# Two first blocks of a short convolution on TensorE, W_in swapped across partitions by TensorE, dummy products during the loads, and two more short blocks

## Chip, cores and metric

The kernel runs on one core of a Trainium2 chip. The metric is the device time of one execution in microseconds (us); "span" is the length of the one profiled execution and is 1.7 to 2.4 us shorter than the time of the same execution. All runs here are of state fast. Engines: TensorE (PE, with PEld for its weight loads), VectorE (DVE), ScalarE (ACT), GpSimd (POOL), and SyncE (SP), whose queue issues most DMAs.

## The reference

A causal convolution over time with 7 taps, whose weights are a softmax per head (8 heads of 24 channels), and after it a two-layer network with exact gelu:

```python
w = exp(weight - max); w = w / (sum(w) + 1e-9)          # weight: [8, 7]
y[b, s, ch] = sum_k w[head(ch), k] * x_pad[b, s + k, ch] # x: [8, 4096, 192], f32
out = gelu(y.reshape(32768, 192) @ w_in) @ w_out         # w_in: [192, 2048], w_out: [2048, 192]
```

## The kernel before

The tokens are cut into two halves of 16384, one half on partitions 0 to 63 and the other on 64 to 127, and each half into blocks. For each block n, VectorE transposes the input and does the convolution (21 instructions over three channel groups p), TensorE multiplies by W_in (`mm1`), ScalarE applies gelu, TensorE multiplies by W_out (`mm2`, of the block before, interleaved with `mm1`), VectorE copies the result out of PSUM (`evac`), and SyncE's queue stores it.

```python
WS = [256, 256] + [512] * ((HALF - 512) // 512)     # tokens per block
...
def conv(n, k, p):                                  # VectorE, k = 0..6, p = 0..2
    src = ap(xT[n % 2], p * XW + 32 * kt, [[NP * XW, 128], [1, w]])
    if k == 0:
        ins = v.tensor_scalar(a, src, wk, None, ALU.mult)
    else:
        ins = v.scalar_tensor_tensor(dst, src, wk, a, op0=ALU.mult, op1=ALU.add)
...
for n in range(NB):                                 # TensorE
    todo = units(n - 1) if n >= 1 else []           # mm2 of the block before
    for i in range(NSL[n]):
        mm1(n, i)                                   # waits for all of conv(n) at i == 0
        for un in todo[a0:a1]:
            mm2(n - 1, *un)
...
sp.dma_start(wsb[:, :], ap(wt, 0, [[KS, H], [1, KS]])).then_inc(S_WSB, 16)   # SyncE's queue
load(sp, 0, (0, 1)); load(sp, 1, (0, 1))
sp.wait_ge(S_WIN[1], 32)
for hf, c0, c1 in ((1, FC, FM), (0, FM, F)):        # the other half of W_in, SBUF to SBUF
    sp.dma_start(win[other half] <- win[this half]).then_inc(S_WIN[2], 16)   # (abridged)
load(sp, 2)
for n in range(1, NB):
    if n + 2 < NB:
        load(sp, n + 2)
    store(sp, n - 1)                                # waits for evac of block n-1
```

## Time and profile before

| | before |
|---|---|
| time, median of 4 | 703.43 us |
| span of the profiled execution | 702.0 us |
| first `mm1` | 15.8 us |
| VectorE starts block 2, has it ready | 28.08 us, 43.7 us |
| TensorE then works until | 698.6 us |

First, lines of the profile page: busy time per engine, and from its part 4 the chain that ended last as shares of the span.

```profile
span 702.0 us, 24852 instructions
...
PE 675.1 (96%) x11366; PEld 517.8 (74%) x11366; DVE 563.0 (80%) x925; ACT 526.3 (75%) x516; POOL 37.2 (5%) x78
...
PE 91%; DVE 4%; DMA 3%; SPq 1%; issue 1%; POOL 0%; POOLq 0%
```

The windows view gives the busy time of each engine in a stretch, then granted TensorE clock, DMA share and GB/s.

```profile
core 0: us, PE busy (x) PEld busy (x) DVE busy (x) ACT busy (x) POOL busy (x), PEclk, DMA share, GB/s
0.00:16.00 16.00, 1.61 (x10) 1.54 (x12) 10.71 (x31) 2.96 (x4) 6.44 (x15) 1.00 1.08 197
16.00:24.00 8.00, 4.32 (x42) 2.90 (x40) 7.96 (x22) 2.32 (x3) 0.87 (x2) 1.00 1.13 239
24.00:32.00 8.00, 7.14 (x122) 5.45 (x120) 5.10 (x11) 7.45 (x8) 1.01 (x2) 1.00 1.01 212
32.00:45.00 13.00, 9.08 (x180) 8.23 (x178) 13.00 (x21) 6.63 (x8) 0.00 (x0) 1.00 0.11 23
...
100.00:200.00 100.00, 100.00 (x1688) 76.49 (x1686) 83.75 (x135) 78.18 (x78) 4.73 (x10) 1.00 0.53 120
```

From 100 us on TensorE is busy all the time; before 45 us it is not, and up to 32 us the DMA engines are full. The timeline (start, length, instruction, and in brackets the idle time before it and what ended it) shows who sets the start. VectorE:

```profile
23.95 1.26 DVE L303 SCALAR_TENSOR_TENSOR xc<-xT,wcol,acc 128x256 bf16<-128x256 f32 x3
28.08 1.90 DVE L273 STREAM_TRANSPOSE xT<-xin 128x512 f32<-128x512 f32 x3 [2.87 <-DMA xin<-in_x_dram]
30.01 1.75 DVE L296 TENSOR_SCALAR acc<-xT,wcol 128x512 f32<-128x512 f32 x3
31.68 10.02 DVE L303 SCALAR_TENSOR_TENSOR acc<-xT,wcol,acc 128x512 f32<-128x512 f32 x15
41.62 2.07 DVE L303 SCALAR_TENSOR_TENSOR xc<-xT,wcol,acc 128x512 bf16<-128x512 f32 x3
```

And TensorE, same view:

```profile
43.83 0.82 PE L423 MATMUL hp<-xc,win 64*128 64x512 bf16 x6 [2.05 <-DVE xc L303]
```

TensorE waits until VectorE has block 2 ready at 43.7 us and is the limit from there to the end. An earlier first matmul is worth something only if it moves such a ready time.

### The profile page before, as it was taken

The numbers are of one execution on the slowest core, as the hardware profiler recorded it, in microseconds if no ns is written. First come the engines' busy times: TensorE is split into PE (matmuls) and PEld (weight loads), VectorE is DVE, ScalarE is ACT, GpSimd is POOL, SyncE is SP. The second block draws the span as 40 slices with busy tenths as digits, with TensorE's granted clock in tenths as the row PEclk, the third lists the DMA queues.
The fourth block names the chain that finished last, engine by engine and source line by source line (L and its number), as shares of the span: only waits on it lengthen the run. The fifth ranks groups of instructions, "written<-read, shape, count | busy, mean of one in ns | idle before, by whom it ended". The sixth has DMA issues, their size and how long they took to land.

```text
span 702.0 us, 24852 instructions
## 1 busy us (share of the span) xinstructions
PE 675.1 (96%) x11366; PEld 517.8 (74%) x11366; DVE 563.0 (80%) x925; ACT 526.3 (75%) x516; POOL 37.2 (5%) x78
## 2 busy tenths in 40 slices
PE   1779999999999999999999999999999999999998
PEld 1566777777777777777777777777777777777777
DVE  6899888988888988888988888898888898888811
ACT  1668777777777777777777777777777777777771
POOL 4000000000000000000000000000000000000000
PEclk9999999999999999999999999999999999999999
DMA  9925545565434665334555444556443566543113
GB/s 203 198 64 116 118 85 117 136 135 122 97 84 107 137 136 132 93 88 97 136 136 134 91 101 89 131 135 135 107 96 84 123 135 137 115 97 77 31 47 93
DMA packets 21929, 78.92 MB, mean 112 GB/s; under 512 B 6720, under 2 KB 9920, under 8 KB 17856
## 3 DMA queue, kind: packets, MB, share of 16 engines
q1 hardware_dynamic: 18096, 74.50, 47.2%
q0 software_dynamic: 2896, 1.67, 1.7%
q8 instruction: 89, 1.46, 0.9%
q10 hardware_dynamic: 832, 1.16, 0.6%
q14 instruction: 16, 0.13, 0.1%
HBM read 53.13 MB, written 25.17 MB: 112 GB/s over the span
## 4 chain that ended last, share of the span: by engine, by line
PE 91%; DVE 4%; DMA 3%; SPq 1%; issue 1%; POOL 0%; POOLq 0%
PE ob L455 47%; PE hp L423 44%; DVE acc L303 3%; DMA xin<-in_x_dram 1%; DMA win<-in_moe_w_in_dram 1%; DVE xT L273 0%; DVE xc L303 0%; DVE acc L296 0%; SPq L130 0%; DVE osb L312 0%; POOL win L229 0%; SPq L495 0%; POOL win L236 0%; POOL sel L185 0%; POOL sel L195 0%
## 5 line engine op out<-in xcount | busy, mean ns | idle before, releaser
L380 ACT ACTIVATE gT<-hp 128x1024 bf16<-128x1024 f32 x512 | 523.4, 1024 | 160.4 <-PE hp L423 160.3
L423 PE MATMUL hp<-xc,win 64*128 64x512 bf16 (+1 forms) x3168 | 425.9, 372 | 19.3 <-DVE xc L303 12.9
L455 PEld LDWEIGHTS ob<-wout,gT 64*128 64x128 bf16 x8192 | 369.1, 94 | 101.9
L455 PE MATMUL ob<-wout,gT 64*128 64x192 bf16 x8192 | 428.6, 243 | 0.0
L303 DVE SCALAR_TENSOR_TENSOR acc<-xT,wcol,acc 128x512 f32<-128x512 f32 (+1 forms) x495 | 326.9, 725 | 0.0
L423 PEld LDWEIGHTS hp<-xc,win 64*128 64x128 bf16 x3168 | 162.9, 95 | 74.6 <-issue 19.2
L312 DVE COPY osb<-ob 128x384 f32<-128x384 f32 x128 | 70.2, 550 | 126.9 <-PE ob L455 126.9
L303 DVE SCALAR_TENSOR_TENSOR xc<-xT,wcol,acc 128x512 bf16<-128x512 f32 (+1 forms) x99 | 66.6, 726 | 0.0
L273 DVE STREAM_TRANSPOSE xT<-xin 128x512 f32<-128x512 f32 (+1 forms) x99 | 60.7, 664 | 3.1 <-DMA xin<-in_x_dram 3.1
L296 DVE TENSOR_SCALAR acc<-xT,wcol 128x512 f32<-128x512 f32 (+1 forms) x99 | 57.1, 629 | 1.2
L223 POOL COPY xT<-xT 128x558 f32<-128x558 f32 x33 | 21.5, 652 | 611.4 <-DVE xT L273 611.4
L214 POOL COPY xT<-xT 128x18 f32<-128x18 f32 x29 | 11.6, 400 | 0.0
L394 PE MATMUL ob<-wnm,sel 8*128 8x7 f32 x6 | 1.4, 354 | 4.2 <-DVE wnm L258 4.2
L394 PEld LDWEIGHTS ob<-wnm,sel 8*128 8x128 f32 x6 | 1.4, 321 | 4.2 <-issue 4.2
L356 ACT ACT_TABLE_LOAD x1 | 1.3, 1283 | 1.7 <-PEq L521 1.7
L250 DVE TENSOR_REDUCE wmx<-wsb 8x1 f32<-8x7 f32 x1 | 0.1, 148 | 2.2 <-DMA wsb<-in_weight_dram 2.2
L262 DVE COPY wcol<-ob 128x21 f32<-128x21 f32 x1 | 0.2, 181 | 1.6 <-PE ob L394 1.6
L229 POOL DMA_DIRECT2D win<-in_moe_w_in_dram x2 | 1.4, 688 | 0.0
L380 ACT ACT_TABLE_LOAD x1 | 1.3, 1283 | 0.0
L236 POOL DMA_DIRECT2D win<-in_moe_w_in_dram x2 | 1.2, 627 | 0.0
L240 POOL DMA_DIRECT2D wout<-in_moe_w_out_dram x1 | 1.2, 1192 | 0.0
L254 DVE TENSOR_SCALAR wsm<-wsm 8x1 f32<-8x1 f32 x1 | 0.1, 142 | 1.1 <-ACT wex L356 1.1
(12 smaller groups left out, 3.3 us busy)
## 6 DMA issues: line engine op xcount, KB each, us to landing
xin<-in_x_dram SPq DMA_DIRECT2D x124, 380.0 KB, 7.1
out_dram<-osb SPq DMA_DIRECT2D x120, 192.0 KB, 3.1
out_dram<-osb SPq DMA_DIRECT2D x24, 48.0 KB, 1.7
wout<-in_moe_w_out_dram POOLq DMA_DIRECT2D x1, 768.0 KB, 13.0
xin<-in_x_dram ACTq DMA_DIRECT2D x4, 188.0 KB, 4.5
xin<-in_x_dram SPq DMA_DIRECT2D x4, 188.0 KB, 4.8
win<-in_moe_w_in_dram POOLq DMA_DIRECT2D x2, 336.0 KB, 8.4
win<-win SPq DMA_DIRECT2D x2, 336.0 KB, 6.3
```

The source lines that it names most:

```text
L214: g.tensor_copy(dst, ap(xT[(n - 1) % 2], WS[n - 1] + 31, [[NP * XW, 128], [XW, NP], [32, HB]],),).then_inc(S_HALO)
L223: g.tensor_copy(ap(xT[n % 2], 1, [[NP * XW, 128], [XW, NP], [32, HB], [1, 31]]), ap(xT[n % 2], WS[n], [[NP * XW, 128], [XW, NP], [32, HB], ...
L229: g.dma_start(ap(win, 64 * hf * NP * F, [[NP * F, 64], [F, NP], [1, FC]]), ap(wint, 0, [[F, 64], [64 * F, NP], [1, FC]]),).then_inc(S_WIN[ ...
L273: v.transpose(ap(xT[n % 2], p * XW + HL, [[NP * XW, 128], [1, w]]), ap(xin[n % NX], 64 * p, [[TB // 32 * D, 128], [D, w // 32], [1, 32]],) ...
L296: ins = v.tensor_scalar(a, src, wk, None, ALU.mult)
L303: ins = v.scalar_tensor_tensor(dst, src, wk, a, op0=ALU.mult, op1=ALU.add)
L312: v.tensor_copy(ap(osb[m % 2], g * C, [[8 * C, 128], [4 * C, 2], [1, C]]), ap(ob[(G0[m] + g) % 2], 0, [[1024, 128], [512, 2], [1, C]]),).t ...
L356: a.activation(out=wex[:, :], in_=wsb[:, :], func=AF.Exp, bias=wmx[:, 0:1], accum_out=wsm[:, 0:1],).then_inc(S_ACTP)
L380: a.activation(out=ap(gT[n % 2], i * c * 2 * w, dst), in_=ap(hp[u % 2], 0, src), func=AF.Gelu,).then_inc(S_GELU)
L394: ins = t.matmul(ob[0][:, p * KS : (p + 1) * KS], sel[:, p * 128 : (p + 1) * 128], wnm[:, :],)
L423: ins = t.matmul(hp[u % 2][:, hf * TB + cc * w : hf * TB + cc * w + w], win[r, p * F + f0 : p * F + f0 + 128], xc[n % 2][r, p * TB : p * T ...
L455: ins = t.matmul(ob[gg % 2][:, 512 * sub : 512 * sub + C], gT[m % 2][r, c0 : c0 + 128], wout[r, i * C : (i + 1) * C], start=(ph == 0 and i ...
```

## The change

Its intent is to use the idle first 45 us better. The convolution of blocks 0 and 1 becomes TensorE products with diagonal matrices (7 per channel group and half); the half of W_in that each partition half lacks is fetched by TensorE products with an identity and copied out of PSUM by VectorE, in place of DMAs; 22 dummy products run while the first loads are under way. Blocks 2 and 3 also shrink from 512 to 256 tokens, and the softmax is computed on all 128 partitions. Core of the diff, with cuts marked by `...`:

```diff
-    WS = [256, 256] + [512] * ((HALF - 512) // 512)
+    WS = [256] * 4 + [512] * ((HALF - 1024) // 512)
+    ND = 2
...
+            def diag(p):                                     # VectorE
+                v.tensor_tensor(dg, idn, wcol, ALU.mult)     # abridged
+            def dup_out(s):                                  # VectorE, 4 x
+                v.tensor_copy(win[.., FH + s * FQ ..], DUPB[s])   # abridged
...
+            late = {(0, 0): (2, 18), (0, 1): (3, 8), (1, 0): (3, 20), (1, 1): (4, 6)}
+            late.update({(2, 0): (4, 13), (2, 1): (4, 21)})   # (block, group): evac before (block, op)
...
+            t.wait_ge(S_WARM, 1)                             # TensorE
+            for i in range(22):
+                t.matmul(hp[1][:, 0:512], warm[:, 0:128], warm[:, :])
+            def dup(s): ...      # win halves times identity, into PSUM
+            def pconv(n, p): ... # 7 taps x 2 halves: dg[..] times xTb[..], into PSUM
+            pconv(0, 0)
+            pconv(0, 1)
+            dup(0)
+            pconv(0, 2)
+            behind = {1: [(dup, 1)], 2: [(dup, 2)], 3: [(dup, 3)]}  # after mm1(0, i)
+            for p in range(NP):
+                behind[4 + p] = [(pconv, 1, p)]
...
-            sp.dma_start(wsb[:, :], ap(wt, 0, [[KS, H], [1, KS]])).then_inc(S_WSB, 16)
+            sp.dma_start(wsb[:, :], ap(wt, 0, [[0, 128], [1, H * KS]])).then_inc(S_WSB, 16)
             load(sp, 0, (0, 1))
-            load(sp, 1, (0, 1))
-            sp.wait_ge(S_WIN[1], 32)
-            for hf, c0, c1 in ((1, FC, FM), (0, FM, F)):
-                sp.dma_start( ... win <- win ... ).then_inc(S_WIN[2], 16)
+            sp.wait_ge(S_WIN[0], 32)
+            load(sp, 1)
             load(sp, 2)
+            sp.wait_ge(S_WOUT, 16)
             for n in range(1, NB):
                 if n + 2 < NB:
                     load(sp, n + 2)
                 store(sp, n - 1)
```

The loop on SyncE's queue is unchanged: block 4's load stands behind the stores of block 0. The table `late` fixes where in VectorE's program each evacuation stands.

## The prediction

> **What bounds the kernel now.** From about 44 us on, TensorE: the windows view gives PE 100% busy in every 100 us stretch from 100 to 600 us, at 20.95 us per 512-token block. Before that VectorE sets the start: the chain of waits runs through input DMA, then VectorE's third convolution (28.08 to 43.7 us), and from 43.83 us through TensorE alone until 698.6 us; evacuation and store add 3.4 us. The first gelu matmul starts at 15.8 us, but only blocks 0 and 1 profit. So the end is "VectorE finishes block k's convolution" plus TensorE's remaining work: 43.8 + 31 x 20.95 + 5.2 = 698.5. The change is worth only what it moves these ready times.
>
> **What changes.** Removed from VectorE: 42 convolution steps on 256 columns (9.5 us per block with transposes). Added: three diagonal builds (est. 0.6 us each, from 0.40 us at 256 columns and 0.68 at 512), four weight copies out of PSUM (est. 0.9 us each, from 0.47 at 384), casts and copies. The W_in swap by DMA (336 KB x 2, 6.3 us) goes; the same DMA engines carry all early loads (the Trainium skill, "DMA: Bandwidth & Descriptors", Issuing engines are not separate DMA queues; the trace agrees: 190 to 277 GB/s shared until 32 us), so inputs land sooner. But blocks 2 and 3 shrink to 256: together 19 us on VectorE where one 512 block costs 15.5.
>
> **Estimated timeline.** First gelu matmul at 11.2 us. Block 0 then waits for weight copies; block 1's last convolution copy ends about 21.5 us, by which time block 2's input should have landed (before: 28.06). Call VectorE's start of block 2 s = 21.5. With evacuations, block 2 is ready at s+10, block 3 at s+20.5. Block 4's load stands behind the stores of block 0, which wait for an evacuation placed inside block 3: it issues about s+16 and needs 8.1 us (measured: first issue 48.9, last landing 57.0). VectorE waits 3 to 4 us; block 4 is ready at s+41 = 62.7. TensorE's work left is then 30 x 20.95 + 5.2 = 633.7, ending at 696.4.
>
> TensorE runs dry near 53 us and idles 9 us. The Trainium skill, "TensorE: Matmul & The Clock Gate", Part 1, says that an idle window of about 3.4 us halves the clock until about as long a busy time; the trace has the first 12 matmuls after idling take 1.46 us where 0.83 is usual. Estimated cost 1 to 2 us. The dummy products let the first matmuls run warm, under 1 us and off the later chain.
>
> Net: -6.6 (earlier s), +0.5 (short blocks), +3.5 (late load), +1.5 (cold clock): -1, or better where these overlap. From block 6 on nothing changes.
>
> **Prediction: 701.5 us**, 8 in 10 between 697.0 and 705.0. Faster by over 2%: 0.01; within 2%: 0.97; slower by over 2%: 0.02.
>
> **Right if:** first gelu matmul at 10 to 13 us; VectorE's first transpose of block 2 at 20 to 24; a VectorE wait for input of 2 to 6 us before block 4's transposes; a TensorE gap of 6 to 12 us ending at 60 to 65, released by VectorE's convolution; then 20.95 us per block, unchanged.
>
> **Wrong if:** weight halves land after 13 us (s goes to 25, the end past 704); block 4's load lands in time (3 to 4 us better); PSUM copies or diagonal builds cost twice my estimate; W_out lands after 23 us and stalls block 1.

## The result, and the profile after

The changed kernel takes 709.16 us (median of 4, 707.68 to 709.73); before it is 703.43. The ratio is 1.0079, with a 95% interval from 1.0061 to 1.0096. (Ratios here are the mean time of one kernel's fast runs over the mean of the other's in the same rounds, so not quite the ratio of the medians quoted.) It is slower by under 1%, and outside the range of 697 to 705.

The page of the kernel after:

```profile
span 706.7 us, 25342 instructions
...
PE 687.9 (97%) x11586; PEld 521.2 (74%) x11586; DVE 558.5 (79%) x924; ACT 528.4 (75%) x523; POOL 39.0 (6%) x90
...
PE 92%; DVE 5%; DMA 2%; issue 1%; SPq 0%; ACT 0%; ACTq 0%
```

Its windows view (columns as above):

```profile
0.00:16.00 16.00, 11.72 (x96) 6.68 (x98) 5.99 (x16) 6.04 (x12) 7.15 (x23) 0.89 0.95 180
16.00:24.00 8.00, 6.55 (x102) 4.48 (x102) 5.10 (x11) 5.42 (x6) 1.22 (x4) 1.00 0.98 175
...
32.00:45.00 13.00, 12.93 (x276) 12.02 (x274) 12.96 (x33) 9.42 (x10) 0.87 (x2) 1.00 0.36 91
45.00:60.00 15.00, 13.61 (x294) 13.17 (x289) 10.44 (x19) 10.45 (x11) 1.01 (x2) 1.00 0.52 120
60.00:100.00 40.00, 32.36 (x473) 22.00 (x470) 37.83 (x61) 27.06 (x28) 2.01 (x4) 0.91 0.57 124
100.00:200.00 100.00, 100.00 (x1686) 75.24 (x1684) 82.64 (x134) 78.39 (x77) 4.74 (x10) 1.00 0.50 116
```

TensorE is far busier before 45 us (6.3 of the 11.7 us in the first row are dummies), nothing of note differs from 100 us on, and there is a new loss between 45 and 100 us: VectorE works only 10.44 of 15 us, TensorE 32.36 of the next 40, at a mean clock of 0.91. The timeline of VectorE shows the first part of it:

```profile
25.78 1.09 DVE L396 STREAM_TRANSPOSE xT<-xin 128x256 f32<-128x256 f32 x3
...
45.10 1.27 DVE L426 SCALAR_TENSOR_TENSOR xc<-xT,wcol,acc 128x256 bf16<-128x256 f32 x3
50.90 1.90 DVE L396 STREAM_TRANSPOSE xT<-xin 128x512 f32<-128x512 f32 x3 [4.53 <-DMA xin<-in_x_dram]
```

VectorE starts block 2 at 25.78 us (before: 28.08), is done with block 3 at 46.37 us, and then waits 4.53 us for block 4's input. SyncE's queue, same view, shows why that was late; L185 is the stores, L171 the load:

```profile
33.58 7.75 SPq L185 DMA_DIRECT2D out_dram<-osb  x8
41.38 1.81 SPq L171 DMA_DIRECT2D xin<-in_x_dram  x4
```

The load is issued right after the stores of block 0, whose second group waits for an evacuation at 39.03 us. TensorE in the same view runs dry in the meantime:

```profile
68.05 1.46 PE L611 MATMUL hp<-xc,win 64*128 64x512 bf16 x6 [7.64 <-DVE xc L426]
```

These six matmuls take 1.46 us, where the same six took 0.82 us in the kernel before at 43.83 us. The windows view with finer stretches shows the clock there, and around the first convolutions:

```profile
10.00:11.00 1.00, 0.91 (x16) 0.91 (x18) 0.23 (x1) 0.68 (x3) 0.84 (x3) 0.94 1.10 145
11.00:14.00 3.00, 3.00 (x36) 2.21 (x32) 0.96 (x1) 0.77 (x2) 0.00 (x0) 0.50 1.39 246
...
66.00:72.00 6.00, 3.95 (x30) 2.48 (x32) 5.96 (x10) 1.55 (x2) 1.00 (x2) 0.50 0.73 168
72.00:73.00 1.00, 1.00 (x16) 0.53 (x12) 1.00 (x3) 0.55 (x2) 0.00 (x0) 0.83 1.07 243
```

The granted clock is 0.50 between 11 and 14 us and from 66 to 72 us. The first of these stretches meets the opening convolutions, which come 2.54 us after the last dummy:

```profile
1.26 6.29 PE L535 MATMUL hp<-warm 128*128 128x512 bf16 x22 [1.26 <-DVE warm L316]
10.09 1.82 PE L575 MATMUL ob<-xTb,dg 64*64 64x256 bf16 x22 [2.54 <-ACT xTb L493]
```

The theory from this: the end is a chain of (1) VectorE's start of block 2, (2) its work up to block 4, (3) the late load, (4) TensorE's remaining work from block 4 on, (5) with a stretch at half clock. Rivals were that the wait is slack and something steady got slower; that the short blocks or the W_in swap are the cost; and that the slow matmuls are no matter of clock.

### The profile page after: what moved, and what is told of

The parts are those of the page before. It is cut to its first block, busy times and chain, and to the rows that moved or that the text cites. A ratio compares the mean times of both kernels' runs of the same rounds, so it can differ in the third digit from the quotient of the medians.

```text
span 706.7 us, 25342 instructions
## 1 busy us (share of the span) xinstructions
PE 687.9 (97%) x11586; PEld 521.2 (74%) x11586; DVE 558.5 (79%) x924; ACT 528.4 (75%) x523; POOL 39.0 (6%) x90
## 4 chain that ended last, share of the span: by engine, by line
PE 92%; DVE 5%; DMA 2%; issue 1%; SPq 0%; ACT 0%; ACTq 0%
PE ob L643 46%; PE hp L611 45%; DVE acc L426 2%; DMA xin<-in_x_dram 1%; PE ob L575 1%; DVE xT L396 1%; DMA wsb<-in_weight_dram 1%; DVE acc L419 1%; DVE xc L426 0%; DVE osb L435 0%; DVE dg L357 0%; SPq L185 0%; SPq L171 0%; DVE win L367 0%; PE ob L551 0%
## 5 line engine op out<-in xcount | busy, mean ns | idle before, releaser
L643 PEld LDWEIGHTS ob<-wout,gT 64*128 64x128 bf16 x8192 | 363.9, 94 | 106.5 <-issue 2.5
L426 DVE SCALAR_TENSOR_TENSOR acc<-xT,wcol,acc 128x512 f32<-128x512 f32 (+1 forms) x480 | 316.9, 722 | 0.0
L426 DVE SCALAR_TENSOR_TENSOR xc<-xT,wcol,acc 128x512 bf16<-128x512 f32 (+1 forms) x96 | 64.5, 723 | 0.0
L289 POOL COPY xT<-xT 128x18 f32<-128x18 f32 x29 | 11.5, 396 | 0.0
L575 PE MATMUL ob<-xTb,dg 64*64 64x256 bf16 x84 | 6.8, 321 | 2.8 <-ACT xTb L493 2.5
L575 PEld LDWEIGHTS ob<-xTb,dg 64*64 64x64 bf16 x84 | 5.2, 126 | 4.4 <-ACT xTb L493 3.0
L535 PE MATMUL hp<-warm 128*128 128x512 bf16 x22 | 6.3, 454 | 1.3 <-DVE warm L316 1.3
L367 DVE CAST win<-ob 128x768 bf16<-128x768 f32 x3 | 2.9, 952 | 4.3 <-PE ob L551 4.3
L535 PEld LDWEIGHTS hp<-warm 128*128 128x128 bf16 x22 | 2.4, 114 | 4.6 <-issue 1.9
(35 smaller groups left out, 20.4 us busy)
## 6 DMA issues: line engine op xcount, KB each, us to landing
wout<-in_moe_w_out_dram POOLq DMA_DIRECT2D x1, 768.0 KB, 15.6
```

The lines of the kernel that those rows point to most:

```text
L289: g.tensor_copy(dst, ap(xT[(n - 1) % 2], WS[n - 1] + 31, [[NP * XW, 128], [XW, NP], [32, HB]],),).then_inc(S_HALO)
L367: v.tensor_copy(ap(win, FH + s * FQ, [[NP * F, 128], [F, NP], [1, FQ]]), ap(DUPB[s], 0, [[1024, 128], [FQ, NP], [1, FQ]]),).then_inc(S_DUPE)
L535: t.matmul(hp[1][:, 0:512], warm[:, 0:128], warm[:, :])
L575: ins = t.matmul(b[r, o : o + w], dg[r, d0 : d0 + 64], xTb[n][r, x0 : x0 + w], start=(k == KS - 1), stop=(k == 0), tile_position=(64 * hf, ...
L643: ins = t.matmul(ob[gg % 2][:, 512 * sub : 512 * sub + C], gT[m % 2][r, c0 : c0 + 128], wout[r, CH[i] * C : (CH[i] + 1) * C], start=(ph == ...
```

## The experiments

Eleven kernels ran, all correct. "Start of block 2", "wait" (VectorE, for block 4's input) and "block 4" (TensorE's first matmul of it) are from each profile's timeline, "end" is the start of the last evacuation, all in us. The column "rest" is end minus block 4, that is, TensorE's work from there on.

The experiments ran in three sessions on three chips: a, b, d, e; then c, f, g, j; then m, k, l. The kernel before ran in each of them, with medians of 704.15, 704.00 and 703.36 us. So a difference between medians of two sessions can be off by 0.8 us; the ratios don't have this fault, and where they say something else it is noted. Where a difference is read from profiles, it is one execution against one.

| run | median (runs) | ratio to before | start of block 2 | wait | block 4 | end | rest |
|---|---|---|---|---|---|---|---|
| before | 703.43 (4) | 1 | 28.08 | | | 698.65 | |
| after | 709.16 (4) | 1.0079 | 25.78 | 4.53 | 68.05 | 703.23 | 635.2 |
| m_again | 709.05 (5) | 1.0083 | 24.30 | 4.80 | 66.83 | 702.38 | 635.6 |
| a_ahead | 702.87 (5) | 0.9993 | 24.39 | none | 62.04 | 697.71 | 635.7 |
| e_keepwarm | 705.94 (5) | 1.0027 | 24.30 | 4.5 | 66.44 | 699.53 | 633.1 |
| j_ahead_keep | 701.70 (5) | 0.9969 | 24.31 | none | 62.83 | 695.93 | 633.1 |
| f_blocks | 703.08 (5) | 0.9993 | 25.07 | none | | 697.39 | |
| b_warm33 | 708.52 (5) | 1.0062 | 24.31 | 4.9 | 66.93 | 703.15 | 636.2 |
| c_warm0 | 711.11 (4) | 1.0102 | 26.09 | 5.81 | 69.64 | 705.38 | 635.7 |
| d_wsbfirst | 709.30 (5) | 1.0076 | 25.21 | 5.5 | 68.44 | 703.33 | 634.9 |
| g_swapdma | 716.71 (4) | 1.0179 | 32.21 | 5.50 | 75.46 | 711.06 | 635.6 |
| k_wsbrow | 707.73 (5) | 1.0056 | 23.52 | 4.96 | 66.20 | 702.06 | 635.9 |
| l_best | 700.16 (5) | 0.9953 | 22.79 | none | 60.79 | 693.88 | 633.1 |

### m_again: the changed kernel once more

No edit. Expected:

> The changed kernel itself once more, on the same chip as the two runs beside it. Its first profile had the opening convolutions at half clock (VectorE's block 2 at 25.8 us); three variants with the same opening did not (24.3 us). If that is chance from execution to execution, its times scatter over some 2 us between 707.5 and 710, and this profile has block 2 at 24.3 or 25.8 us, with the same 4.5 to 5.5 us wait for block 4's input and half clock after it.

Measured: 708.18 to 709.86, and block 2 at 24.30 us. TensorE's and VectorE's timelines:

```profile
1.26 7.76 PE L535 MATMUL hp<-warm 128*128 128x512 bf16 x22 [1.26 <-DVE warm L316]
10.08 1.39 PE L575 MATMUL ob<-xTb,dg 64*64 64x256 bf16 x22 [1.07 <-ACT xTb L493]
```

```profile
24.30 1.09 DVE L396 STREAM_TRANSPOSE xT<-xin 128x256 f32<-128x256 f32 x3
```

So of two profiles of one program, one has the opening convolutions at half clock and one has not, and that is worth 1.5 us of block 2's start. The timelines show where they part: the 22 dummies took 7.76 us here and 6.29 us in the first profile (633 against 379 ns each in the median), so the gap between them and the convolutions was 1.07 us here and 2.54 us there. The wait (4.80 us) and the half clock before block 4 are in both. The times spread over 1.7 us here and from 707.68 to 709.73 us in the first result; how many of these executions opened at half clock is not known, for only one of each set was profiled.

### a_ahead: the input loads one block earlier

```diff
+            load(sp, 3)
             for n in range(1, NB):
-                if n + 2 < NB:
-                    load(sp, n + 2)
+                if n + 3 < NB:
+                    load(sp, n + 3)
                 store(sp, n - 1)
```

> The changed kernel, with every input load from block 4 on issued one block earlier, ahead of the stores that it stood behind. Theory (a chain: VectorE start of block 2, late load of block 4, cold TensorE clock): VectorE's 4.5 us wait for block 4's input goes, block 4 is ready at about 63.4 us instead of 67.9, TensorE's gap shrinks from 7.6 to about 3 us and the half-clock stretch after it mostly goes; time falls by 4.5 to 6 us, to about 703 to 704.5. Rival 1 (the steady state or TensorE's own start is the limit, and the wait is slack): within 1 us of 709. Rival 2 (the earlier load collides with other transfers and another wait takes its place): the wait goes, but less than 3 us is gained.

Measured: 702.87, 6.2 us less than m_again, at the upper edge of what was expected and a little beyond; the spans of the two profiles differ by 4.3 us. The wait is gone (VectorE's line has no idle time before it), and TensorE's gap is 4.59 us in place of 7.6 to 8.2. VectorE first, then TensorE:

```profile
44.90 1.89 DVE L396 STREAM_TRANSPOSE xT<-xin 128x512 f32<-128x512 f32 x3
```

```profile
62.04 1.47 PE L611 MATMUL hp<-xc,win 64*128 64x512 bf16 x6 [4.59 <-DVE xc L426]
```

The wait was on the chain; that is shown, and the rest from block 4 on is as before (635.7 against 635.6 us in m_again), so the gain lies ahead of block 4. One part of the expectation failed: the half clock did not go with the shorter gap. The windows view of this run has it still:

```profile
60.00:62.00 2.00, 0.00 (x0) 0.00 (x0) 2.00 (x4) 0.00 (x0) 0.00 (x0) 0.62 0.42 114
62.00:66.00 4.00, 3.96 (x30) 2.49 (x32) 3.96 (x7) 1.56 (x2) 1.01 (x2) 0.50 0.83 183
66.00:68.00 2.00, 2.00 (x22) 1.03 (x18) 2.00 (x4) 1.10 (x2) 0.00 (x0) 0.67 1.02 219
```

### e_keepwarm: dummy products in the gap before block 4

```diff
+                if i == 0 and n == 4:
+                    for _ in range(30):
+                        t.matmul(hp[u % 2][:, 0:512], warm[:, 0:128], warm[:, :])
                 if i == 0:
```

> The changed kernel with 30 dummy products on TensorE put into its gap before block 4 (about 6.5 us of the 7.6 us gap). Theory: the half clock from 65.5 to 72.3 us in the records costs about 1.6 us of TensorE work on the chain; with the gap filled the clock stays full and the time falls by 1.2 to 1.8 us to about 707.5. Rival: the slow matmuls after the gap are a start-up effect of the block or wait on other engines; no change (709), or worse by the overlap if the dummy products outlast the gap.

Measured: 705.94, 3.1 us less than m_again (3.9 us by the ratios), about twice what was expected or more. TensorE's timeline and then the windows view of this run:

```profile
58.99 6.65 PE L601 MATMUL hp<-warm 128*128 128x512 bf16 x30
66.44 0.82 PE L614 MATMUL hp<-xc,win 64*128 64x512 bf16 x6 [0.81 <-DVE xc L426]
```

```profile
62.00:66.00 4.00, 3.63 (x17) 1.47 (x15) 4.00 (x7) 0.00 (x0) 0.00 (x0) 1.00 0.59 136
66.00:72.00 6.00, 5.56 (x78) 3.28 (x80) 5.96 (x11) 4.70 (x5) 1.00 (x2) 1.00 0.90 209
```

The six matmuls take 0.82 us again, the clock stays at 1.00, and the rest from block 4 on is 633.1 us in place of 634.9 to 636.2 us in the eight profiles without filled gaps (after, m_again, a, b, c, d, g, k). So the half clock costs 1.8 to 3.1 us here, 2.1 in the first profile after. The clock record gives the same size by another way. Take TensorE's busy time from block 4 on in windows of 0.5 us, times the share of the clock that was not granted: the sum is 2.1 us in the first profile after, 1.9 to 2.8 us in all eight, and zero in e_keepwarm. The last evacuation starts at these times in the view of the chain (start, length, what), m_again first and then e_keepwarm:

```profile
702.38 0.56 DVE osb L435
```

```profile
699.53 0.56 DVE osb L435
```

The Trainium skill, "TensorE: Matmul & The Clock Gate", Part 1 (What's actually happening), names the mechanism, a clock halved after idling; pace, record and remedy agree with it.

### j_ahead_keep: both repairs

The edits of a_ahead and e_keepwarm, with 18 dummies.

> Both repairs together: input loads one block earlier, and 18 dummy products (3.9 us) in the 4.6 us gap that TensorE still has before block 4. The first run with earlier loads still showed half clock from 60.8 to 67.4 us. Theory: the two costs add up, so the time falls by a further 3 us from 702.9, to 699.5 to 700.5, below the kernel before. Rival: they overlap or the steady state takes it back; 702 or more.

Measured: 701.70, ratio 0.9969 (0.9957 to 0.9982): below the kernel before, but 1.2 us above the expected band. The dummies outlast the gap by 0.8 us (block 4 ready at 62.0, first matmul at 62.83). The two gains add up in large part: 7.4 us together against 9.3 for the sum of the two alone (8.0 and 10.2 by the ratios), and 6.5 against 7.5 us in the ends of the profiles. The surplus dummies are 0.8 us of what is missing; the other 0.2 to 1.4 us can be overlap or scatter.

### f_blocks: the block sizes of before

```diff
-    WS = [256] * 4 + [512] * ((HALF - 1024) // 512)
+    WS = [256] * 2 + [512] * ((HALF - 512) // 512)
...
-            late = {(0, 0): (2, 18), (0, 1): (3, 8), (1, 0): (3, 20), (1, 1): (4, 6)}
-            late.update({(2, 0): (4, 13), (2, 1): (4, 21)})
-            for n in range(3, NB):
+            late = {(0, 0): (2, 12), (0, 1): (2, 20), (1, 0): (3, 16), (1, 1): (4, 0)}
+            for n in range(2, NB):
```

> The changed kernel with two 256-token blocks and then 512 (as before), instead of four, evacuations placed to suit; load order as in the changed kernel. Theory: block 4's late load disappears (the load after block 0's stores is then wanted only some 16 us later); VectorE starts block 2 at 24.3 to 25.8 us and has it ready 16.5 us later, at 41 to 42.5; 654.9 us of TensorE work follow. TensorE runs dry for 3 to 5 us before it, with up to 3 us of half clock. Time 700.5 to 705, that is 4 to 8 us below the changed kernel. Rival (the short blocks 2 and 3 themselves help by feeding TensorE in smaller pieces): 708 or more.

Measured: 703.08, as expected. VectorE starts block 2 at 25.07 us, TensorE's block 2 starts at 42.11 us:

```profile
42.11 1.46 PE L610 MATMUL hp<-xc,win 64*128 64x512 bf16 x6 [4.31 <-DVE xc L426]
```

With two long blocks in place of four short ones the same load order costs nothing, since the load behind the stores is wanted some 15 us later (VectorE takes block 4 at 59.70 us, and would have taken it at 44.9 us in m_again). The half clock is here too, but shorter: after the gap of 4.31 us it costs 1.3 us by the clock record. So the late load and the short blocks are one cause: the shorter blocks brought the need forward, and the load order did not follow. This is also the change without its block sizes: level with the kernel before (0.9979 to 1.0006).

### b_warm33 and c_warm0: more dummies, no dummies

`range(22)` becomes `range(33)`, or the loop goes.

> The changed kernel with 33 dummy products instead of 22, so that they end at about 9.95 us, just before the first convolution matmul at 10.1. Theory: the first three convolutions and the first weight swap ran at half clock (0.215 us a pair of matmuls against 0.11 later) because TensorE had been idle from 7.55 to 10.09; bridged, they run at 0.11, block 0's first gelu matmul comes some 2 us earlier (12.4 instead of 14.5), and VectorE starts block 2 about 2 us earlier, so the time falls by about 2 us to 707. Rival: the half clock is a property of these small 64x64 products, not of the idle time; then their pace stays 0.21 and the time stays 709.

> The changed kernel without the 22 dummy products. Theory: the first convolutions run at half clock in every execution (1.7 us for 16 matmuls instead of 1.04), where the changed kernel has it only in some (its profile did, three later runs with the same opening did not); VectorE starts block 2 at 25.5 to 27 us instead of 24.3, and the time is 709 to 711. Rival (dummy products are of no use, as other waits hide them): 708 to 709, with the same start of block 2 at 24.3 us.

Measured: with 33, 708.52; without, 711.11. The timeline of TensorE without dummies shows the first convolutions slow:

```profile
10.24 2.56 PE L573 MATMUL ob<-xTb,dg 64*64 64x256 bf16 x22 [10.24 <-ACT xTb L493]
```

and with 33 shows them fast:

```profile
10.09 1.39 PE L575 MATMUL ob<-xTb,dg 64*64 64x256 bf16 x22 [0.21 <-ACT xTb L493]
```

(The first profile after, with 22, has 1.82 us here, turning to half clock midway.) So the 22 dummies are worth 2 us by the medians and 1.3 us by the ratios; without them block 2 starts at 26.09 us, in its band, and the time is 0.1 us above its own. The theory that small products are slow in themselves is out, since the same 22 take 1.39 us in b_warm33 and in m_again. That 33 are better than 22 is not shown: 708.52 against 709.05, with intervals that overlap (1.0048 to 1.0076 and 1.0069 to 1.0096); the expected 2 us did not come.

### d_wsbfirst and k_wsbrow: the convolution weights

They landed at 4.85 us, where the kernel before had them at 2.17. In d_wsbfirst all other opening loads wait for them; in k_wsbrow they come as one row and TensorE spreads them:

```diff
-            sp.dma_start(wsb[:, :], ap(wt, 0, [[0, 128], [1, H * KS]])).then_inc(S_WSB, 16)
+            sp.dma_start(wsb[:, :], ap(wt, 0, [[H * KS, 1], [1, H * KS]])).then_inc(S_WSB, 16)
...
+                if i == 2:
+                    t.wait_ge(S_ONE, 1)
+                    t.wait_ge(S_WSB, 16)
+                    t.matmul(ob[1][:, 960 : 960 + H * KS], one[:, :], wsb[:, :]).then_inc(S_WBC)
```

> The changed kernel, with all other opening loads held back until the convolution weights have landed. Tells why these landed at 4.85 us where the kernel before had them at 2.17. Theory Q (the 128-partition copy shares the DMA engines with the loads issued right behind it): alone it lands at 2.2 to 2.8 us, softmax and diagonals finish 2 us earlier, the first convolution matmul starts at about 8 us right after the dummy products and runs at full clock, VectorE starts block 2 at 21 to 22 us instead of 25.8, and the time falls by 3 to 5 us, to 704 to 706. Rival O (the replicated copy of 128 rows of 224 B is slow by itself): it still lands at 4.5 us or later, everything else slips behind it by 3 us, and the time does not fall.

> The changed kernel, with the convolution weights loaded as one row of 224 bytes and spread over the partitions by one TensorE product with ones, in place of a load that writes 128 rows. Theory: the 128-row load is slow by itself (it took 3.1 us alone, the 8-row load before 1.4), so the softmax starts at about 3.0 us instead of 4.85 and the first convolution matmul at about 8.5 us, where the dummy products still keep the clock up in every execution. But block 1's input, which landed at 18.4 us, becomes the next limit, so that VectorE starts block 2 only 0.5 to 1.5 us earlier than 24.3; time 706.5 to 708.5. Rival (nothing else limits): the whole 1.8 us come through, and in every execution, time 705 to 706.5.

Issue to landing of this load, in the view of its tile: first after, then d_wsbfirst.

```profile
DMA to landing us min/median/max: 4.0/4.0/4.0
```

```profile
DMA to landing us min/median/max: 3.1/3.1/3.1
```

Alone it still takes 3.1 us, so most of it is its own and 0.9 us comes from the loads beside it. Neither expectation of d_wsbfirst is met to the letter: it landed at 3.98, between the two bands; the time (709.30) did not fall: the weights were there 0.87 us earlier, but GpSimd's masks, held back too, came 0.89 us after they were wanted. As one row the weights are spread by TensorE at 2.65 us, and the softmax starts at 3.36:

```profile
2.65 0.67 PE L544 MATMUL ob<-wsb,one 1*128 1x56 f32 x2
```

k_wsbrow gains 1.3 us on m_again (707.73; same session, the intervals just touch) and starts block 2 at 23.52 us, in the band. What limits it now is not block 1's input, which had been expected: the dummies, begun cold, end only at 9.37 us and hold up the first convolution, which starts at 9.30.

### g_swapdma: the W_in halves by DMA again

`dup` and `dup_out` go; SyncE's queue copies a quarter of the columns when the first piece of W_in is there, and the rest after it has issued block 1's loads:

```diff
             sp.wait_ge(S_WIN[0], 32)
+            swap(0, FQ, S_SW[0])
             load(sp, 1)
+            sp.wait_ge(S_WIN[1], 32)
+            swap(FQ, FH, S_SW[1])
             load(sp, 2)
```

> The changed kernel with the W_in halves swapped by DMA as before (in two pieces), in place of TensorE and VectorE; all else as changed. Theory: the swap on TensorE saves the DMA time but puts four copies of 0.96 us and their waits into the opening chain; by DMA the second piece lands at about 19 us, so slices 2 to 7 of block 0 come later (19 instead of 16.1), yet VectorE is free of the copies; VectorE starts block 2 at 24 to 26 us as now, and the time is 707 to 711, within 2 us of the changed kernel: the swap's place is worth little. Rival (the swap on TensorE is what brings the early start): VectorE's block 2 starts at 28 us or later, 712 or more.

Measured: 716.71, so the rival holds: block 2 starts at 32.21 us. TensorE's timeline:

```profile
16.82 1.73 PE L577 MATMUL hp<-xc,win 64*128 64x256 bf16 x24 [2.52 <-DMA win<-win]
23.11 4.04 PE L577 MATMUL hp<-xc,win 64*128 64x256 bf16 x36 [4.56 <-DMA win<-win]
```

The second piece lands at 23.1 us and block 1's input at 20.4 (in m_again VectorE took it at 18.31 us without a wait). Part of the loss is half clock again: 0.50 from 18 to 28 us, around the wait for the second piece. In this order of loads the swap on TensorE is worth 7.7 us (6.8 by the ratios); another order of the DMAs was not tried, so the figure is no price of the swap as such.

### l_best: what helped, together

a_ahead, k_wsbrow, 13 dummies before block 4, and W_out's load issued after block 1's input has landed.

> Everything that helped, together: loads one block earlier, 13 dummy products before block 4 (18 outlasted the gap by 0.9 us), weights as one row, and W_out's load issued after block 1's input has landed. Theory: VectorE starts block 2 at about 23 us, block 4 is ready at about 60.7 us, 633 us of TensorE work at full clock and 3.4 us of tail follow: span about 697, time 698.5 to 700. Rival: the later W_out stalls block 1's second product, or the load order makes a new wait; 701 or more.

Measured: 700.16, ratio 0.9953 (0.9941 to 0.9966), just above its band. Block 4 starts at 60.79 us, as expected:

```profile
60.79 0.82 PE L625 MATMUL hp<-xc,win 64*128 64x512 bf16 x6 [0.23 <-DVE xc L433]
```

It beats both kernels, by 0.5% and by 1.3%. What the later W_out adds by itself is not told apart.

## Why the prediction was wrong

The chain was the right one, and the direction of its net was not. The prediction's terms, in us, beside the first profile after:

| term | predicted | measured | difference |
|---|---|---|---|
| VectorE starts block 2 (s) | 21.5 | 25.78 | +4.3 |
| blocks 2 and 3 on VectorE | 20.5 | 20.6 | +0.1 |
| wait for block 4's input | 3.5 | 4.53 | +1.0 |
| block 4 on VectorE, to TensorE's start | 17.2 | 17.15 | 0 |
| TensorE's rest at full clock | 633.7 | 633.1 (e_keepwarm) | -0.6 |
| half clock before and in block 4 | 1.5 | 2.1 | +0.6 |
| TensorE's end | 697.9 | 703.2 | +5.3 |

- The step that failed is "block 1's last convolution copy ends about 21.5 us". Of the 4.3 us, 1.5 are the opening convolutions at half clock (25.78 against 24.30 in m_again), which the prediction ruled out: "The dummy products let the first matmuls run warm". They ran out at 7.55 us, 2.5 us before the convolutions. Of the other 2.8, about 1.5 go when the weights come as one row and loads and W_out are reordered (22.79 in l_best, 0.8 of it in k_wsbrow). The replicated weight load was not costed at all.
- The last 1.3 us of that step have a place but no shown cause: in l_best the first gelu matmul came at 11.54 us (predicted 11.2), and from it to VectorE's start of block 2 it was 11.25 us where the prediction allowed 10.3. That stretch takes 11.2 to 11.5 us in every profile with four short blocks and the swap on TensorE, so in the first profile after 3.3 of the 4.3 us were lost before the first gelu matmul. VectorE's new work was estimated well (a diagonal 0.57 us, a weight copy 0.96; estimates 0.6 and 0.9); what the rest of the 11.25 us waits for no run takes apart.
- "VectorE waits 3 to 4 us" for block 4's input was right in mechanism and 1 us short: the load went out at s + 15.6 us, as predicted (s + 16), but took 9.5 us to land where 8.1 was reckoned. a_ahead shows that the wait was on the chain. It was between 4.5 and 5.8 us in all runs with that load order and the four short blocks.
- "Estimated cost 1 to 2 us" for the clock was right in mechanism and too small; 1.8 to 3.1 us. The half clock lasted 3.7 (d) to 5.7 us (k) after TensorE resumed, where the prediction reckoned with about 3.4.
- "First gelu matmul at 11.2 us": 14.52 in this profile, 13.04 in m_again. "TensorE gap of 6 to 12 us" was right (7.64), its end at 68 in place of 60 to 65 follows from s. "From block 6 on nothing changes" was right.
- The terms as predicted sum to 697.9 us, which with the tail of 3.4 and the 1.9 between span and time of the profiled execution before is 703.2; the prediction's own net, -1.1 us, gives 702.3. The quoted 701.5 took off another 0.8 to 1.7 us "where these overlap". For the wait and the half clock, a_ahead, e_keepwarm and j_ahead_keep leave 0.2 to 1.4 us for an overlap; the other terms were not tested for one, so that step was a guess.
- "Within 2%" was right, with 0.8% slower.

In one sentence: the change brought VectorE to block 2 between 2.3 and 3.8 us earlier, and gave back 4.5 to 4.8 us in a load that now came too late and 2.1 to 2.5 us in the half clock that TensorE's longer gap brought on.

## What to carry to other kernels

When a change speeds up the start or shortens the first blocks, look at every load that stands behind a store or another wait in the same queue: it was early enough for the old pace only, and moving it up one block took three changed lines here. A gap on TensorE can cost the gap and then a stretch at half pace after it (here after gaps of 4.3 to 8.2 us), so compare the same matmul's duration before and after a gap, and count the two apart. And check that dummy products meant to bridge a wait last until that wait ends in the trace: in the opening here a rest of 2.54 us was followed by half clock, and one of up to 1.94 us was not.

## What the Trainium skill lacked or had wrong

- "TensorE: Matmul & The Clock Gate", section Why this matters for your kernels, advises no idle gaps over about 3 us. Here shorter ones were enough: after 2.54 us idle (7.55 to 10.09) the clock went to half at 10.9 us in the first profile after, and likewise at 11.1 us after 2.66 us in g_swapdma; after 1.0 to 1.9 us (f, m_again, e, a, d, j) it did not. So the advice is too wide, and the reason given there, a window of idle, does not cover it: the 3.4 us before 10.9 us held 0.8 us of matmuls. Whether the small 64x64 products count as full activity is not told apart. The page's free-running window of about 3.4 us fits in another way: the record's stretches at half clock last 3.4 us (first profile after, 10.9 to 14.3), 6.8 us (same, 65.5 to 72.3) or 10.2 us (m_again, 61.7 to 71.9).
- The same page works out the cost of half clock for a kernel that waits in every K-tile (HAM oscillation), but has no measured cost of a single gap in a dense kernel: 1.8 to 3.1 us of TensorE's work here, on top of the gap, for gaps of 4.6 to 8.2 us.
- The same page's caveats on clock records could add this: the granted clock reads 1.00 in the opening of c_warm0 (10 to 13 us), though 22 convolution matmuls take 2.56 us in place of 1.39. The pace of the matmuls was the surer reading there.
- "DMA: Bandwidth & Descriptors" has no figure for a small load that replicates one row: 128 rows of 224 bytes took 3.1 us alone and 4.0 us beside other loads; as one row, issued at the same 0.81 us, the weights were in use at 2.65 us.
